# Pairs 6 to 11 of an SSD scan in 32x64 array tiles, a block's two pairs finished together

## The chip, the core and the metric

The kernel runs on one core of one Trainium2 chip, as one launch. A core has a matrix engine (TensorE, PE in the profile, with weight loads listed apart as PEld), VectorE (DVE), ScalarE (ACT), GpSimd (POOL) and a queue that issues most of the transfers (SP). The metric is the device time of one execution in microseconds, the median of several runs. Less is better.

## The reference

Two layers follow each other. The first is a chunked state-space scan over 4 batches x 8 heads x 768 tokens, head dimension 32, state dimension 16. The second is a gated feed-forward layer over all 3072 tokens, 256 -> 1536 -> 256.

```python
# scan, per batch and head, in chunks of 32 tokens (state starts at zero)
cum = cumsum(log(a[chunk]))
M = (Cc @ Bc.T) * exp(cum_i - cum_j) * causal
y = M @ xc + (Cc @ state) * exp(cum)
state = exp(sum(log a)) * state + sum_j(Bc_j xc_j exp(cum_end - cum_j))
# feed-forward over the tokens; the 8 heads x 32 make the 256 features
out = (relu(y @ w_gate) * (y @ w_val)) @ w_out
```

## The kernel before

The kernel takes chunks of 128 tokens, 6 per batch (`NC`). Two chunks are a pair of 256 tokens; there are 12 pairs, 0 to 11, three per batch (`PPB`). Two pairs make a block of 512 tokens, and the feed-forward layer runs over 6 blocks (b = 0 to 5). The decay is folded into B and C, which are scaled by factors from products of `a` that run over a whole pair. So inside a pair a token's output is a masked product of scaled C and B with x, plus scaled C times the carried state.

The scan of one pair p consists of these steps. The names are those of the profile.

- `scale` (L355): GpSimd scales B and C to bf16 and casts x (`to_x`, tile xb). From pair 6 on (`NDMA`) it is `scale_padded` (L278): B and two copies of C go to a tile bz of 6 blocks of 128 columns, each copy of C zero outside the states of its half of the heads, and one DMA transpose from the SP queue turns the six blocks (tile TT). Before pair 6 TensorE transposes do that. Heads are numbered h = 4t + q here: q is one of four 32-row strips of the array, t the half of the strip.
- `G` (L435): the products of C and B. Per chunk four matmuls, one per 32-row strip, each 32x128 in size with 256 moving columns, into four PSUM banks g0 to g3.
- `gevac` (L449): the four banks go, causally masked, to the bf16 tile gs: g0 and half of g1 by ACT (L455, L463) with a mask by GpSimd (L169), the rest by DVE (L466, L470).
- `inter` (L575, matmuls L595): the carried state. Per chunk two full 128x128 matmuls with 128 moving columns into the bank y. The state stands as a block-diagonal tile Sm.
- `Dm` (L599, matmuls L606): gs times x, 16 matmuls per pair in 128x32 tiles, added to the same bank y.
- `yevac` (L613, copies L304): bank y to the bf16 tile yT, by ACT.
- `states` (L532, matmuls L545): the state sums over B and x in the bank A_ps, 4 matmuls per chunk in 128x32 tiles, and `spread` (L553, `spread_one` L509, DVE L514 to L522), which makes Sm from them. Within a batch the sum runs on in PSUM; at the fifth chunk it is multiplied by `over` and continues as `carry`.

The feed-forward layer of block b has 12 slices of 128 hidden features. `gv` (L627) does one slice for 512 tokens: two matmuls of 512 columns for gate (L631), two for val (L634), a relu by ACT (L637) and a product by DVE (L638) into h. `gvh_mm` (L640), `gvh_relu` and `gvh_mul` do the same for 256 tokens, a half tile (L649, L656, L659). `fout` (L671, matmuls L678) multiplies h with w_out, 12 matmuls of 256 columns for 128 tokens, into the bank o, and `foevac` (L696) copies o out (ACT, L706) and issues the store (SP, L707).

PSUM has eight banks: five `shared` ones that gate, val, gv, g0 to g3 and o take in turn, and one each for the tags y, tp and Aps. In the transposes' time tp holds their results.

`in_order` (L15) fixes the order of the instructions on each engine to that of the program, so the loop over b (L859 on) is the schedule. With P = 2b+2, Q = 2b+3 and W = 2b+1 its order from b = 1 on is this:

1. Half tiles for slices 0 to `nh`-1 of the first 256 tokens (`nh` is 6 in block 1, 5 in later ones). At one of them the second pair W of the block is finished: `inter(W)`, `Dm(W)`, `states(P)`, `yevac(W)`, `spread(P)` (L878 to L888). Then half tiles of the same slices for the second 256 tokens.
2. Full `gv` for the remaining slices; `scale` of later pairs on GpSimd.
3. `inter(P)`, `fout(b, 0)`, `G(P)`, `gevac(P)`, `fout(b, 1)`, `foevac`, `fout(b, 2)`.
4. `Dm(P)`, `states(Q)`, `yevac(P)`, `G(Q)`, `spread(Q)`, `gevac(Q)`, `fout(b, 3)`, `foevac` (L962 to L976).

So pair P, the first half of block b+1, is ready a fourth of a block's output work before block b+1 starts, and its partner Q is finished inside block b+1, behind the half tiles of that block's first half.

Of the kernel before, what the change touches and what calls it, by code (L numbers as in the profile page):

```python
# [29 lines left out]
def kernel(  # L30
# [219 lines left out]
    over = const.tile([128, NB], FP32)  # L250

# [13 lines left out]

    yT = glob.tile([128, 2, T], BF16)
# [5 lines left out]
    def zero_padded():  # L272
        for n in range(3):
            z = glob.tile([128, 6, 128], BF16, name="bz%d" % n)
            nc.gpsimd.memset(z, 0.0)
            turned.append(z)

    def scale_padded(p, eng):  # L278

        b, c0, _ = place(p)  # L280
        z = turned[p % 3]
        dst = z.rearrange("s (i k) (q t n) -> s i k t q n", k=3, q=4, t=2)
        src = st[p]["bcr"].rearrange("s i j (t q) n -> s i j t q n", t=2)
        f = fac[:, b, c0:c0 + 2]
        for t in range(2):
            for j in range(2):
                eng.tensor_tensor(  # L287
                    out=dst[:, :, j * (1 + t), t], in0=src[:, :, j, t],
                    in1=f[:, :, j, 4 * t:4 * t + 4].to_broadcast([128, 2, 4, N]), op=ALU.mult)
        st[p]["B"] = [z[:, 3 * i] for i in range(2)]  # L290
        tt = st[p]["TT"] = att.tile([128, 6, 128], BF16, tag="TT", name="TT")
        nc.sync.dma_start_transpose(out=tt, in_=z.rearrange("s k n -> s (k n)"))
# [110 lines left out]
    def bt(p, i, rows):  # L403
        return st[p]["TT"][rows, 3 * i] if p >= NDMA else st[p]["BT"][rows, i]

    def ct(p, i, rows=slice(0, 128), t=None):
        if p >= NDMA:
            c = st[p]["TT"][rows, 3 * i + 1:3 * i + 3]
        elif p < NWIDE:
# [25 lines left out]
    def G(p):  # L435
        s = st[p]
        if "gp" not in s:
            G_banks(p)
        g = s["gp"]
        for i in range(2):  # L440
            for q in range(4):
                r = slice(32 * q, 32 * q + 32)
                nc.tensor.matmul(  # L443
                    out=split(p, g[q][:, i]), lhsT=bt(p, i, r), rhs=ct(p, i, r),
                    start=(i == 0), stop=True, tile_position=(32 * q, 0),
                    skip_group_check=True)
        s["gs"] = att.tile([128, 4, 4, 128], BF16, tag="gs", name="gs", bufs=2)

    def gevac(p, half=True, early=False, between=None, after={}):  # L449
# [19 lines left out]
        if half and not early:  # L469
            nc.vector.tensor_tensor(out=d[:, 1, 0:2], in0=g[1][:, 0:2], in1=m[:, 0:2],  # L470
                                    op=ALU.mult)

# [151 lines left out]

    fst = {}

    def gv(b, f):  # L627
        tk = slice(b * 512, (b + 1) * 512)
        g, v = bank("gate"), bank("val")
        for k in range(2):  # L630
            nc.tensor.matmul(out=g, lhsT=w_tile(wgs, f, k), rhs=yT[:, k, tk],  # L631
                             start=(k == 0), stop=(k == 1))
        for k in range(2):
            nc.tensor.matmul(out=v, lhsT=w_tile(wvs, f, k), rhs=yT[:, k, tk],  # L634
                             start=(k == 0), stop=(k == 1))
# [60 lines left out]
    def foevac(b, ts):  # L696
# [5 lines left out]
        if last:  # L702
# [4 lines left out]
        nc.sync.dma_start(  # L707
            out=out[r0 - 128:r0 + 128, :].rearrange("(i p) m -> p i m", p=128), in_=ob)
# [91 lines left out]
    def turn(p):  # L800
        if p >= NDMA:
            return
        transp(p, 1)
        transp(p, 0)

    def tevac(p, beng, *cengs):
        if p >= NDMA:
            return
# [47 lines left out]
    scale_bc(3, nc.gpsimd)  # L856
    to_x(2, nc.gpsimd)

    for b in range(NBLK):  # L859
        P, Q, W = 2 * b + 2, 2 * b + 3, 2 * b + 1  # L860
        more = P < NPAIR
        for n in (P + 2, P + 3):
            if b and n < NPAIR:
                load(n, nc.sync)

        nh = (4, 6, 5)[min(b, 2)]
        if b == 1:
            zero_padded()
        for f in range(nh):
            if b == 0:  # L870
                continue
            turning = f == (3 if b == 1 else 2)
# [5 lines left out]
            if turning:  # L878
# [3 lines left out]
                if more:  # L882
                    states(P)
                if b == 1:
                    scale_one(P, nc.gpsimd, 1)
                yevac(W, nc.scalar)
                if more:
                    spread(P)  # L888
        for f in range(nh):
            gvh(b, f, 1)  # L890
        for f in range(nh, NF):
            gv(b, f)
# [13 lines left out]
            elif more:  # L906
                if f == max(5, nh):
# [3 lines left out]
                if f == 8:  # L911
                    turn(Q)
                    tevac(Q, nc.scalar, nc.vector)
                    if Q + 1 < NPAIR:
                        scale(Q + 1, nc.gpsimd)
        if more and b:
            inter(P, 0)
            inter(P, 1)
        if b == 0:
# [30 lines left out]
            inter(P, 1)  # L950
        else:
            fout(b, 0)
            foevac(b, 0)
            if more:
                G(P)
                gevac(P)
# [4 lines left out]
        if more:  # L961
            Dm(P)  # L962
            states(Q)
            if b == 0:
                yevac(P, nc.vector)
                G(Q)
                gevac(Q, after={3: lambda: spread(Q)})
                new_bs(Q + 1)
                scale_one(Q + 1, nc.gpsimd, 0)
            else:  # L970
                yevac(P, nc.scalar)
                G(Q)
                spread(Q)
                gevac(Q)
            fout(b, 3, range(6, NF) if b == 0 else range(NF))
            foevac(b, 3)  # L976
        else:
            fout_last(b)
# [32 lines left out]
```

## Time and profile before

| what | value |
|---|---|
| runs before | 123.75, 124.55, 124.83 us; median 124.55 us |
| profiled execution, its own time | 123.81 us |
| its span, first to last instruction | 122.1 us |
| granted TensorE clock | 1.0 |
| DVE, ACT, POOL busy | 74%, 63%, 39% of the span |
| full gate and val matmuls (L631, L634) | 84 + 84, 25.0 us busy each |
| half tile matmuls (L649) | 240, 23.1 + 23.0 us busy |
| output matmuls (L678) | 276, 33.0 us busy |
| DMA transposes (L292) | 6, median 3.0 us from issue to landing |

The profile is of one execution; its own time is 0.74 us below the median of the runs. A matmul's row gives its duration from start to result (273 ns for 256 columns), but matmuls follow each other faster than that, and a group's busy time counts overlapping ones once; the cost of a group is read from the start of it to the start of the next. Blocks 2 to 5 run from 49.2 to about 119 us.

### The profile page before, as it was taken

The page shows a single profiled execution, that of the slowest core. Times are in us where ns is not written, and L with a number is a line of the kernel's source. Part 1 is how long each engine was busy: PE and PEld are TensorE (multiplying, and loading weights), DVE is VectorE, ACT ScalarE, POOL GpSimd, SP SyncE. Part 2 cuts the span into 40 slices and gives each one's busy share as a digit, 9 for nine tenths or more (in the row PEclk, how much of TensorE's full clock was granted, in tenths as well). Part 3 has the DMA queues.
Part 4 walks back from the last instruction along what each step waited for, and adds up shares of the span by engine and source line. Part 5 has one row for each costly group of instructions (what it writes and reads, how often), then busy time and mean ns, then how long its engine had stood idle before and what let it go on. Part 6 is the DMA issues. An engine that isn't in the chain of part 4 may idle for free.

```text
span 122.1 us, 3384 instructions
## 1 busy us (share of the span) xinstructions
PE 118.1 (97%) x1253; PEld 81.5 (67%) x1253; DVE 90.9 (74%) x224; ACT 77.2 (63%) x175; POOL 47.3 (39%) x99
## 2 busy tenths in 40 slices
PE   7999999999999999999999999999999999999990
PEld 2656854677885577884577874677864678854790
DVE  5978879986999855898765998756897657788500
ACT  4167886750988735787645886545987347886240
POOL 6879999043875071904132706033600033000000
PEclk9999999999999999999999999999999999999999
DMA  3999999989979899598962499932320002200022
GB/s 63 209 186 142 180 194 193 213 138 120 166 74 198 111 105 157 177 98 111 128 136 94 107 113 113 162 74 86 116 40 0 0 0 91 86 0 0 0 87 90
DMA packets 79024, 13.31 MB, mean 109 GB/s; under 512 B 71856, under 2 KB 79008, under 8 KB 79008
## 3 DMA queue, kind: packets, MB, share of 16 engines
q1 hardware_dynamic: 71520, 10.15, 51.7%
q0 software_dynamic: 4080, 2.36, 13.7%
q10 hardware_dynamic: 3408, 0.59, 2.5%
q8 instruction: 10, 0.16, 0.6%
q14 instruction: 6, 0.05, 0.1%
HBM read 11.12 MB, written 3.15 MB: 117 GB/s over the span
## 4 chain that ended last, share of the span: by engine, by line
PE 94%; DVE 3%; issue 0%; DVEq 0%
PE o L678 25%; PE gv L649 22%; PE val L634 15%; PE gate L631 15%; PE w L198 4%; PE g L443 3%; PE y L606 3%; PE y L595 2%; PE o L690 1%; PE tp L375 1%; DVE gs L466 1%; DVE bs L330 1%; PE A_ps L545 1%; PE bt L424 1%; PE dw L234 0%; DVE CT L401 0%
## 5 line engine op out<-in xcount | busy, mean ns | idle before, releaser
L638 DVE TENSOR_TENSOR h<-r,val 128x512 bf16<-128x512 bf16 x42 | 28.6, 686 | 6.5 <-ACT r L637 5.5
L678 PE MATMUL o<-wo,h 128*128 128x256 bf16 x276 | 33.0, 273 | 0.0
L637 ACT ACTIVATE r<-gate 128x512 bf16<-128x512 f32 x42 | 25.1, 597 | 9.3 <-PE gate L631 8.8
L678 PEld LDWEIGHTS <-h 128*128 128x128 bf16 x276 | 25.9, 98 | 4.9 <-issue 1.9
L169 POOL TENSOR_SCALAR_AFFINE_SELECT gs<-gs 128x512 bf16<-128x512 bf16 (+1 forms) x24 | 12.2, 529 | 35.3 <-ACT gs L455 35.3
L659 DVE TENSOR_TENSOR h<-r,gv 128x256 bf16<-128x256 bf16 x60 | 23.7, 418 | 2.7 <-ACT r L656 2.1
L634 PE MATMUL val<-yT,wv 128*128 128x512 bf16 x84 | 25.0, 379 | 0.0
L631 PE MATMUL gate<-yT,wg 128*128 128x512 bf16 x84 | 25.0, 379 | 0.0
L656 ACT ACTIVATE r<-gv 128x256 bf16<-128x256 f32 x60 | 22.8, 386 | 2.1
L649 PE MATMUL gv<-yT,wg 128*128 128x256 bf16 x120 | 23.1, 273 | 0.0
L649 PE MATMUL gv<-yT,wv 128*128 128x256 bf16 x120 | 23.0, 273 | 0.0
L466 DVE TENSOR_TENSOR gs<-g,masks 128x512 bf16<-128x512 f32 x24 | 15.4, 684 | 5.2 <-PE g L443 5.2
L634 PEld LDWEIGHTS <-wv 128*128 128x128 bf16 x84 | 8.1, 98 | 10.0 <-DMA wv<-in_moe_w_val_dram 0.3
L455 ACT CAST gs<-g 128x512 bf16<-128x512 f32 x12 | 7.1, 588 | 12.1 <-PE g L443 12.0
L287 POOL TENSOR_TENSOR bz<-bcr,fac 128x128 bf16<-128x128 f32 x24 | 8.9, 402 | 11.6 <-DMA bcr<-in_B_dram 8.0
L631 PEld LDWEIGHTS <-wg 128*128 128x128 bf16 x84 | 8.1, 98 | 7.9
L649 PEld LDWEIGHTS <-wv 128*128 128x128 bf16 x120 | 11.7, 98 | 1.3
L649 PEld LDWEIGHTS <-wg 128*128 128x128 bf16 x120 | 11.2, 98 | 1.8 <-issue 0.2
L706 ACT COPY ob<-o 128x512 f32<-128x512 f32 x11 | 6.5, 587 | 6.3 <-PE o L678 6.3
L304 ACT CAST yT<-y 128x512 bf16<-128x512 f32 (+1 forms) x12 | 6.3, 541 | 5.7 <-PE A_ps L545 3.4
L304 POOL CAST xb<-xr 128x512 bf16<-128x512 f32 (+1 forms) x10 | 5.9, 592 | 5.8 <-DMA xr<-in_x_dram 5.8
L198 PE MATMUL w<-const-bfloat16-1.0 128*128 128x128 bf16 (+2 forms) x27 | 6.3, 378 | 0.8 <-PEq L995 0.8
(109 smaller groups left out, 107.1 us busy)
## 6 DMA issues: line engine op xcount, KB each, us to landing
xr<-in_x_dram SPq DMA_DIRECT2D x23, 128.0 KB, 3.2
out_dram<-ob SPq DMA_DIRECT2D x11, 256.0 KB, 2.3
bcr<-in_B_dram SPq DMA_DIRECT2D x16, 64.0 KB, 2.9
bcr<-in_C_dram SPq DMA_DIRECT2D x16, 64.0 KB, 2.8
wg<-in_moe_w_gate_dram POOLq DMA_DIRECT2D x6, 128.0 KB, 4.9
wv<-in_moe_w_val_dram POOLq DMA_DIRECT2D x6, 128.0 KB, 5.0
wo<-in_moe_w_out_dram POOLq DMA_DIRECT2D x3, 256.0 KB, 7.0
bcr<-in_C_dram SPq DMA_DIRECT2D x3, 128.0 KB, 5.7
```

The lines of the kernel that those rows point to most:

```text
L169: nc.gpsimd.affine_select(out=dst, in_=dst, pattern=pattern, compare_op=ALU.is_ge, fill=0.0, base=0, channel_multiplier=-1)
L198: nc.tensor.matmul(out=w[:, 0:cols], lhsT=nc.const_aps.tensor(1.0, [128, 128], BF16), rhs=nc.const_aps.tensor(1.0, [128, cols], BF16), sta ...
L304: (eng.copy if eng is nc.scalar else eng.tensor_copy)(out=out, in_=in_)
L466: nc.vector.tensor_tensor(out=d[:, q], in0=g[q], in1=m, op=ALU.mult)
L631: nc.tensor.matmul(out=g, lhsT=w_tile(wgs, f, k), rhs=yT[:, k, tk], start=(k == 0), stop=(k == 1))
L634: nc.tensor.matmul(out=v, lhsT=w_tile(wvs, f, k), rhs=yT[:, k, tk], start=(k == 0), stop=(k == 1))
L637: nc.scalar.activation(r, g, AF.Relu)
L638: nc.vector.tensor_tensor(out=fst[b][:, f], in0=r, in1=v, op=ALU.mult)
L649: nc.tensor.matmul(out=gv_[:, j], lhsT=w_tile((wgs, wvs)[j], f, k), rhs=yT[:, k, tk], start=(k == 0 and not (early and j)), stop=(k == 1), ...
L656: nc.scalar.activation(r[:, 0:256], fst[b, f, u][:, 0], AF.Relu)
L659: nc.vector.tensor_tensor(out=fst[b][:, f, u * 256:(u + 1) * 256], in0=fst.pop((b, f, u, "r"))[:, 0:256], in1=fst.pop((b, f, u))[:, 1], op ...
L678: nc.tensor.matmul(out=o[:, ts % 2], lhsT=fst[b][:, f, ts * 128:(ts + 1) * 128], rhs=wo[:, f], start=(f == 0 and new), stop=(f == NF - 1), ...
```

## The change

Pairs 6 to 11 get another layout and another place; pairs 0 to 5 keep theirs.

- `scale_padded` now writes B, C and the two copies of C, 8 blocks instead of 6, with the heads in their natural order (h = 2q + t), in one multiplication and two copies. The transpose turns 8 blocks.
- `G_rows` replaces `G` for these pairs: 16 matmuls instead of 8, each in a 32x64 tile. `inter_rows` replaces `inter`: per chunk four matmuls in 32x64 tiles with 128 columns instead of two full ones. The state then needs no block-diagonal tile, but 64 columns with a mask (tile Sn).
- `Dm_two`, `states_two`, `sums_two` and `yevac_two` do both pairs of a block together. `Dm_two` goes head half by head half (k) through two banks, tags y and tp. `yevac_two` has ACT copy the first bank and DVE the second. `states_two` makes each chunk's sum by itself; `sums_two` adds them up on DVE and masks on GpSimd.
- In blocks 2, 3 and 4 the whole scan of the next block's two pairs lies in the output part, and its copies to yT come two output matmuls before the next block starts. From block 3 on there are no half tiles, and the first slice of a block goes k by k (`turns`). Block 2, which still finishes pair 5, has 8 slices in half tiles instead of 5.
- Block 1 gains `over_sum2` on DVE, three small operations behind `spread(4)`. `zero_padded` moves ahead of the loop. Loads of pairs 8, 9, 10 and 11 and the scaling move earlier in program order; the last store of blocks 2 and 3 is split in two.

```diff
+    def over_sum2(de):
+        own = smask.rearrange("p t (q d) -> p q t d", q=4)[:, :, :, 0]
+        prod = const.tile([128, 2, 8], FP32)
+        for n in range(2):
+            nc.vector.tensor_tensor(
+                out=prod[:, n].rearrange("p (q t) -> p q t", t=2),
+                in0=de[:, (2 + n) * 8:(3 + n) * 8].rearrange("p (q t) -> p q t", t=2),
+                in1=own, op=ALU.mult)
+        nc.vector.tensor_reduce(out=over2[:, 2:4], in_=prod, op=ALU.add,
+                                axis=mybir.AxisListType.X)
...
+    def G_rows(p):
...
+        for i in range(2):
+            for o in range(2):
+                for q in range(4):
+                    r, m = slice(32 * q, 32 * q + 32), slice(64 * o, 64 * o + 64)
+                    nc.tensor.matmul(
+                        out=s["gp"][q][m, i], lhsT=tt[r, 4 * i, m],
+                        rhs=tt[r, 4 * i + 2:4 * i + 4], start=(i == 0), stop=True,
+                        tile_position=(32 * q, 64 * o), skip_group_check=True)
...
+    def inter_rows(p, opened):
...
+            for q in range(4):
+                r, o = slice(32 * q, 32 * q + 32), 64 * (q % 2)
+                nc.tensor.matmul(
+                    out=Y[q // 2][o:o + 64, p % 2, i], lhsT=Sm[r], rhs=tt[r, 4 * i + 1],
+                    start=q not in opened, stop=True, tile_position=(32 * q, o),
+                    skip_group_check=True)
...
+    def Dm_two(ps):
+        for k in range(2):
+            for p in ps:
+                x_, gs = st[p]["x"], st[p]["gs"]
+                for i in range(2):
+                    for c in range(4):
+                        h = 4 * k + c
+                        nc.tensor.matmul(
+                            out=Y[k][32 * c:32 * c + 32, p % 2, i],
+                            lhsT=x_[i][:, h * D:(h + 1) * D], rhs=gs[:, h // 2, 2 * i + h % 2],
...
+    def yevac_two(ps):
+        tk = slice(ps[0] * 256, (ps[1] + 1) * 256)
+        for k, eng in ((0, nc.scalar), (1, nc.vector)):
+            copy(eng, yT[:, k, tk], Y[k].rearrange("q u i m -> q (u i m)"))
...
-        nh = (4, 6, 5)[min(b, 2)]
+        nh = (4, 6, 8, 0)[min(b, 3)]
...
                 if b == 1:
...
                     spread(P)
+                    over_sum2(de)
+                else:
+                    sums_two((P, Q))
...
+        elif more:
+            ahead = (P + 2, Q + 2) if Q + 2 < NPAIR else ()
+            fout(b, 0, range(9))
+            G_rows(P)
+            opened = y_banks()
+            inter_rows(P, opened)
+            inter_rows(Q, opened)
+            gevac(P)
+            fout(b, 0, range(9, NF))
+            fout(b, 1)
+            foevac(b, 1)
+            fout(b, 2, range(6))
+            G_rows(Q)
+            gevac(Q)
+            fout(b, 2, range(6, NF))
+            fout(b, 3, range(10))
+            Dm_two((P, Q))
+            states_two(ahead)
+            yevac_two((P, Q))
+            sums_two(ahead)
+            fout(b, 3, range(10, NF))
+            foevac(b, 3)
+            continue
```

More of the change, by code (lines that the diff above doesn't have):

```diff
@@ L625, with gv @@
+    def yevac_two(ps):
+        tk = slice(ps[0] * 256, (ps[1] + 1) * 256)
+        for k, eng in ((0, nc.scalar), (1, nc.vector)):
+            copy(eng, yT[:, k, tk], Y[k].rearrange("q u i m -> q (u i m)"))
+        for p in ps:
+            st.pop(p)
     fst = {}
-    def gv(b, f):
+    def gv(b, f, turns=False):
+        if b not in fst:
+            fst[b] = ffn.tile([128, NF, 512], BF16, tag="h", name="h")
         tk = slice(b * 512, (b + 1) * 512)
         g, v = bank("gate"), bank("val")
[L630 to L635, printed above, removed]
+        order = [(g, wgs, 0), (g, wgs, 1), (v, wvs, 0), (v, wvs, 1)]
+        for o, ws, k in sorted(order, key=lambda e: e[2]) if turns else order:
+            nc.tensor.matmul(out=o, lhsT=w_tile(ws, f, k), rhs=yT[:, k, tk],
+                             start=(k == 0), stop=(k == 1), skip_group_check=True)
@@ L960 @@
             foevac(b, 2)
[L961 to L976, printed above, removed]
-        else:
-            fout_last(b)
+            fout_last(b)
+            continue
+        Dm(P)
+        states(Q)
+        if b == 0:
+            yevac(P, nc.vector)
+            G(Q)
+            gevac(Q, after={3: lambda: spread(Q)})
+            new_bs(Q + 1)
+            scale_one(Q + 1, nc.gpsimd, 0)
+        else:
+            yevac(P, nc.scalar)
+            G(Q)
+            spread(Q)
+            gevac(Q)
+        fout(b, 3, range(6, NF) if b == 0 else range(NF))
+        foevac(b, 3)
     in_order(tc)
```

141 lines of the change are left out of this document (100 added, 41 removed).

## The prediction

> **What bounds the kernel now.** First the page's busy times, its 40 slices and the chain of waits, to see which engine sets the end:
>
> ```profile
> PE 118.1 (97%) x1253; PEld 81.5 (67%) x1253; DVE 90.9 (74%) x224; ACT 77.2 (63%) x175; POOL 47.3 (39%) x99
> PE   7999999999999999999999999999999999999990
> PE 94%; DVE 3%; issue 0%; DVEq 0%
> ```
>
> From 11 us to the last output tiles the chain is TensorE alone: its stream has no hole, at a full clock. So an instruction taken off PE gives back its whole length, and any new wait of PE costs its whole length. Other engines count only where PE begins to wait for them. Next PE's timeline at the end of block 3 and the start of block 4 (start, us, engine, line):
>
> ```profile
> 77.69 0.59 PE L634 MATMUL val<-yT,wv 128*128 128x512 bf16 x2
> 78.12 0.39 PE L595 MATMUL y<-TT,Sm 128*128 128x128 bf16 x4
> 78.34 1.47 PE L678 MATMUL o<-wo,h 128*128 128x256 bf16 x12
> 79.75 0.40 PE L443 MATMUL g<-TT 32*128 32x256 bf16 x8
> 80.08 2.79 PE L678 MATMUL o<-wo,h 128*128 128x256 bf16 x24
> 82.80 0.41 PE L606 MATMUL y<-gs,xb 128*32 128x128 bf16 x16
> 83.04 0.26 PE L545 MATMUL A_ps<-xb,bz 128*32 128x64 bf16 x12
> 83.23 0.40 PE L443 MATMUL g<-TT 32*128 32x256 bf16 x8
> 83.56 1.48 PE L678 MATMUL o<-wo,h 128*128 128x256 bf16 x12
> 84.88 0.38 PE L649 MATMUL gv<-yT,wg 128*128 128x256 bf16 x2
> ...
> 86.19 0.28 PE L595 MATMUL y<-TT,Sm 128*128 128x128 bf16 x2
> 86.40 0.41 PE L606 MATMUL y<-gs,xb 128*32 128x128 bf16 x16
> 86.63 0.29 PE L545 MATMUL A_ps<-xb,bz 128*32 128x64 bf16 x16
> 86.85 0.39 PE L649 MATMUL gv<-yT,wg 128*128 128x256 bf16 x2
> ```
>
> Starts give the prices. Two of 512 columns take 78.12 - 77.69 = 0.43. Twelve of 256 from 84.88 take 1.31: 0.109 each. Four full ones of 128 columns take 78.34 - 78.12 = 0.22: 0.056 each. `Dm` takes 82.80 to 83.04: 16 matmuls go four at a time, four turns of 0.056. `G` goes four at a time too, so two turns of 0.109, and 0.11 of its 80.08 - 79.75 = 0.33 is something else. The same surplus stands wherever the tile shape changes: 79.75 - 78.34 less 12 x 0.109 = 0.10; 83.23 - 83.04 less three chunks of 0.03 = 0.10; 86.85 - 86.63 less four = 0.10. So a change of tile shape costs 0.10.
>
> Last the neighbours that PE may come to wait for: DVE in block 1; the last product of h and the copy to yT in block 3; the transposes on SP's queue.
>
> ```profile
> 34.04 0.42 DVE L522 TENSOR_TENSOR Sm<-A_ps,smask 128x256 bf16<-128x256 f32 x1
> 34.37 0.28 DVE L514 TENSOR_SCALAR carry<-A_ps,over 128x64 f32<-128x64 f32 x1
> 34.68 0.42 DVE L522 TENSOR_TENSOR Sm<-carry,smask 128x256 bf16<-128x256 f32 x1
> 35.02 2.86 DVE L659 TENSOR_TENSOR h<-r,gv 128x256 bf16<-128x256 bf16 x8
> ```
>
> ```profile
> 78.52 0.69 DVE L638 TENSOR_TENSOR h<-r,val 128x512 bf16<-128x512 bf16 x1 [0.17 <-ACT r L637]
> ```
>
> ```profile
> 83.26 0.58 ACT L304 CAST yT<-y 128x512 bf16<-128x512 f32 x1 [1.08 <-PE y L606]
> ```
>
> ```profile
> 46.47 1.31 SPq L292 DMA_TRANSPOSE TT<-bz  x1
> ...
> 59.49 2.84 SPq L292 DMA_TRANSPOSE TT<-bz  x2
> ```
>
> **What PE saves.** Carried state of pairs 6 to 11: 20 full matmuls x 0.056 = 1.12 become 10 chunks, each one turn of four tiles in different row strips, 0.56: -0.56. Shape changes: seven a block in blocks 2 to 4 (pair W 2, G 2, Dm to G to output 3) and two in block 5, 23 in all; after it 8, 6, 6 and 0, 20 in all: -0.30. State sums: 16 chunk steps become 10, x 0.029: -0.17. Half tiles: a slice costs 8 x 0.109 = 0.874 against 4 x 0.216 = 0.863, and 20 slices become 8: -0.12. `Dm` stays at four turns a pair. `G_rows` stays at two turns if all eight tiles of a chunk run side by side; its later last start (four more starts, some 4 ns apart as inside every group) adds 6 x 0.014 = +0.08. Sum -1.07.
>
> **What PE newly waits for.** At the three block starts. Before, `yevac` ran under half tiles or under `fout(3)`; now the first gate product needs all 512 tokens. ACT's copy began 0.46 behind the first `Dm` matmul (83.26 - 82.80), and in the new order the first bank's half of `Dm_two` is as long as that `Dm`. So yT's first half is there 0.46 + 0.58 + 0.05 (from one engine's end to the next's start) = 1.10 behind it. PE has in that time 0.47 of `Dm_two`, three state steps 0.09, a change 0.10 and two output matmuls 0.22 = 0.88; block 4 has no states, 0.79. Wait 0.22 + 0.22 + 0.31 = +0.75. DVE's copy of the second half starts 0.23 later than ACT's, lasts at most the 0.69 of the other 128x512 operations and is needed 0.43 later, since the slice goes k by k: nothing.
>
> At both `G_rows`, three times. The first begins 9 x 0.109 + 0.10 behind the last val, 78.12 + 1.08 = 79.20; its fourth bank is that of this val, free when the product of 78.52 ends, 79.21 + 0.05: 0.05. The second comes six output matmuls behind `fout(1)`; its fourth bank is the one that `foevac` copies. That copy begins 0.31 behind the last matmul of `fout(1)` (81.60 against 81.29) and ends at 0.90 + 0.05, the tile's turn is at 0.87: 0.07. Sum 3 x 0.12 = +0.35. `Dm_two` follows 16 matmuls behind the second `G_rows`; the last mask on DVE and POOL ended 2.05 behind G's last start in block 3, the tiles that read it start at 2.15: nothing, by a hair.
>
> Block 1. `over_sum2` stands on DVE between the Sm of 34.68 and the eight products from 35.02. Its like in block 0 took 0.34 for one product of 32 elements and 0.10 for the sum; two products and a sum 0.45 to 0.55, say 0.48. The first of the eight frees, at 35.44, the bank of the half tile begun at 33.34, and five banks on PE wants it at 35.54: 0.06 of cover. So +0.42, between 0 (if DVE overlaps them) and 0.50.
>
> Hidden: `sums_two` and the masks (DVE one copy and three sums of 0.25 against two Sm of 0.33 in block 2, where DVE waits for ACT between half tiles; POOL waits 35.3 us in total for the ACT copies); `scale_padded` on POOL (four of 0.36 become, from 0.36 for 128 and 0.58 for 256 elements, one of about 1.0 and two of 0.3); the early memsets (POOL is idle from 21 to 26 us). Without that cover the latter two would cost 0.2 a pair and 3.
>
> Transposes. SP goes from the one at 46.47 (a third longer now) over six loads, two stores and six loads, 0.52 each for the stores and 0.7 to 0.8 for each load, so pair 7's is issued at 57.5 to 59.1, not 59.49. Six blocks landed after 2.7 to 4.1; eight, by 8/6 at most, 2.9 to 5.5. So it lands at 60.4 to 64.6, most likely 61.4. Before, `G(7)` at 65.36 was its first reader; now `inter_rows(7)` is, at about 62.2 (49.6 + 11.2 + 9 output matmuls + 0.4). Taken: 0, since issue and landing have mostly been at their short ends; late end +2.4.
>
> Sum: -1.07 + 0.75 + 0.35 + 0.42 = +0.45. The profiled 123.81 becomes 124.3; it lies 0.74 below the median of the runs, which becomes 125.0. One per cent, 1.25 us, is about what a measurement can tell from no change here.
>
> **Rivals.** (B) The two column halves of a row strip don't run side by side. Rows show strips side by side (L443), column tiles side by side (L606) and both on the diagonal (L586, 32x32, four a turn), but never two column tiles in one strip. Then `G_rows` takes four turns, 6 x 0.22, and the carried state two, 10 x 0.056: +1.87 more, 126.9. Against it: every shape seen overlapped. 0.17.
>
> (C) Pair 7's transpose lands late. From 63.0 on, a wait of 0.8, the kernel is over 1% slower; at 63.2 it is 126.0. For it: the transposes of 86.88 took 4.1 to land on a quieter queue. 0.15.
>
> (D) Tiles of different strips can't write one bank at once; `inter_rows` puts q = 0 and 1 into one. Price 10 x 0.056 = +0.56, 125.5. Against it: L586's 16 matmuls, four strips into one bank, took 13.40 to 13.79 where one by one would be 0.9. 0.05. The Trainium skill, "TensorEngine Tiling (Array Packing)", Gotcha 1: PSUM Pressure, says that different row tiles cannot access the same bank simultaneously. By that rule it would be 125.5; the trace doesn't agree.
>
> (E) The small waits don't come, and `over_sum2` hides: 124.55 - 1.07 + 0.2 to 0.75 = 123.7 to 124.2; only with no wait at all, 123.5. For it: four of my waits are below 0.1. 0.13; over 1% faster 0.05, if changes of shape between small tiles cost less than 0.10.
>
> My forecast has 0.50, own range 124.3 to 125.8. Slower by over 1%: B 0.17, C 0.15 and the upper end of mine 0.04, 0.36; faster 0.05; within 0.59. The range 123.8 to 126.8 leaves out the low half of E and most of B.
>
> **What would show it.** Right: G_rows 0.33 from its start to the next group's besides the carried state, which takes 0.06 a chunk; block 3 some 0.2 shorter than 17.87; a wait of 0.2 to 0.3 before the first gate of blocks 3 to 5; PE 0.4 late at the half tile of 35.54. Wrong: G_rows over 0.5 (B); a hole before `inter_rows` in block 2 (C); no gap at the block starts (E).

## The result, and the profile after

| what | before | after |
|---|---|---|
| median of the runs | 124.15 us (4 runs) | 127.70 us (127.23 to 129.62, 4 runs) |
| ratio, 95% interval | | 1.0271 (1.0220 to 1.0321): slower |
| profiled execution, its own time | 123.81 us | 127.92 us |
| its span | 122.1 us | 126.2 us |

Medians count every run, while ratios, here and below, leave out those of a kernel's runs that took over 1.5% more than its fastest, so a ratio need not be the quotient of two medians.

By the ratio the changed kernel is 3.4 us slower; 0.45 us were forecast, and 127.70 us lies above the range given, 123.8 to 126.8. The page's busy times, its row of TensorE slices and its chain:

```profile
PE 120.2 (95%) x1249; PEld 77.5 (61%) x1249; DVE 89.4 (71%) x214; ACT 74.0 (59%) x160; POOL 52.0 (41%) x105
PE   7899999999999999989989999999999999999990
PE 78%; DMA 6%; SPq 5%; DVE 5%; ACT 2%; issue 1%
```

TensorE has fewer matmuls than before (1249 against 1253) and is still the bound, but its share of the chain fell from 94% to 78%: DMA, SP's queue and DVE are in it now. The view of waits says for what TensorE stood still (us in total, times, longest):

```profile
PE w L198 <- PEq L1134: 0.8, 1, 0.8
PE gv L750 <- ACT yT L316: 0.6, 1, 0.6
PE y L663 <- DMA TT<-bz: 0.5, 1, 0.5
PE tpb L387 <- DVE bs L342: 0.4, 1, 0.4
PE gv L750 <- DVE h L760: 0.2, 1, 0.2
```

The first row is the launch, as long in the kernel before; the fourth is at 5.85 us, ahead of block 0. The timeline shows the other three in their places (start, us, engine, line; idle time and its cause in brackets), and two of the new groups and a block start behind them:

```profile
12.31 0.42 PE L750 MATMUL gv<-yT,wg 128*128 128x256 bf16 x1
12.53 0.37 PE L750 MATMUL gv<-yT,wv 128*128 128x256 bf16 x1
12.73 0.27 PE L750 MATMUL gv<-yT,wg 128*128 128x256 bf16 x1
12.84 0.27 PE L750 MATMUL gv<-yT,wv 128*128 128x256 bf16 x1
...
37.17 0.25 DVE L271 TENSOR_TENSOR prod<-de,smask 128x8 f32<-128x8 f32 x2
37.46 0.17 DVE L275 TENSOR_REDUCE over<-prod 128x2 f32<-128x16 f32 x1
...
38.01 0.38 PE L750 MATMUL gv<-yT,wg 128*128 128x256 bf16 x2 [0.16 <-DVE h L760]
...
55.68 0.29 PE L690 MATMUL A_ps<-xb,bz 128*32 128x64 bf16 x16
...
55.91 0.59 ACT L316 CAST yT<-y 128x512 bf16<-128x512 f32 x1 [0.19 <-PE A_ps L690]
...
56.55 0.38 PE L750 MATMUL gv<-yT,wg 128*128 128x256 bf16 x2 [0.57 <-ACT yT L316]
...
61.91 4.35 SPq L304 DMA_TRANSPOSE TT<-bz  x3
...
64.81 0.29 PE L663 MATMUL y<-TT,Sn 32*64 32x128 bf16 x4
...
65.58 0.30 PE L663 MATMUL y<-TT,Sn 32*64 32x128 bf16 x8 [0.48 <-DMA TT<-bz]
...
83.03 0.48 PE L489 MATMUL g<-TT 32*64 32x256 bf16 x16
83.27 0.40 PE L663 MATMUL y<-TT,Sn 32*64 32x128 bf16 x12
83.61 2.47 PE L779 MATMUL o<-wo,h 128*128 128x256 bf16 x21
...
88.94 0.39 PE L779 MATMUL o<-wo,h 128*128 128x256 bf16 x2
89.38 0.38 PE L735 MATMUL gate<-yT,wg 128*128 128x512 bf16 x1
```

The first four lines are block 0: starts of half tile matmuls are 0.22 apart until 12.7 us and 0.11 after, so the clock was half until there. The record of the granted clock begins, at full, at 12.70 us here and at 6.47 us in the kernel before. At 38.01 TensorE is 0.32 late (start to start, less the 0.218 of two matmuls), at 56.55 0.64, at 65.58 0.64. At 89.38 the block start is 0.22 late.

Where the 4.11 us between the two profiled executions are, by starts of TensorE (a block runs from its first gate or half tile matmul to the next block's, block 5 to the start of the last matmul; differences are of unrounded times):

| | start of block 1 | block 1 | block 2 | block 3 | block 4 | block 5 | last matmul to the end |
|---|---|---|---|---|---|---|---|
| before | 30.94 | 18.24 | 17.84 | 17.87 | 17.78 | 16.29 | 3.15 |
| after | 33.09 | 18.55 | 19.96 | 17.79 | 17.84 | 15.57 | 3.42 |
| difference | +2.15 | +0.32 | +2.11 | -0.08 | +0.06 | -0.72 | +0.27 |

Block 0 and what comes ahead of it hold the same 327 matmuls in both kernels, and yet the largest part is there. Of DMA the page says (issues, KB each, median us to landing):

```profile
xr<-in_x_dram SPq DMA_DIRECT2D x23, 128.0 KB, 3.6
...
bcr<-in_B_dram SPq DMA_DIRECT2D x16, 64.0 KB, 3.5
bcr<-in_C_dram SPq DMA_DIRECT2D x16, 64.0 KB, 3.3
```

Before, these were 3.2, 2.9 and 2.8. The loads are the same in number and size (the page has 11.12 MB read from HBM in both); only those of the later pairs are issued earlier.

### The profile page after: what moved, and what is told of

Its sections match the earlier page's. It is cut to its first block, busy times and chain, and to the rows that moved or that the text cites. A ratio compares the mean times of both kernels' runs of the same rounds, so it can differ in the third digit from the quotient of the medians.

```text
span 126.2 us, 3355 instructions
## 1 busy us (share of the span) xinstructions
PE 120.2 (95%) x1249; PEld 77.5 (61%) x1249; DVE 89.4 (71%) x214; ACT 74.0 (59%) x160; POOL 52.0 (41%) x105
## 3 DMA queue, kind: packets, MB, share of 16 engines
q0 software_dynamic: 4080, 2.36, 13.9%
HBM read 11.12 MB, written 3.15 MB: 113 GB/s over the span
## 4 chain that ended last, share of the span: by engine, by line
PE 78%; DMA 6%; SPq 5%; DVE 5%; ACT 2%; issue 1%
PE o L779 23%; PE gate L735 17%; PE val L735 17%; PE gv L750 7%; SPq L92 3%; DMA bcr<-in_C_dram 3%; DMA TT<-bz 3%; PE w L198 2%; PE g L489 2%; PE g L450 1%; ACT yT L316 1%; PE tp L387 1%; DVE h L760 1%; PE y L628 1%; DVE Sm L544 1%; PE o L791 1%
## 5 line engine op out<-in xcount | busy, mean ns | idle before, releaser
L739 DVE TENSOR_TENSOR h<-r,val 128x512 bf16<-128x512 bf16 x54 | 36.7, 686 | 9.3 <-ACT r L738 6.4
L738 ACT ACTIVATE r<-gate 128x512 bf16<-128x512 f32 x54 | 32.3, 597 | 12.6 <-PE gate L735 11.8
L735 PE MATMUL gate<-yT,wg 128*128 128x512 bf16 x108 | 32.6, 379 | 0.2
L735 PE MATMUL val<-yT,wv 128*128 128x512 bf16 x108 | 32.6, 379 | 0.0
L169 POOL TENSOR_SCALAR_AFFINE_SELECT gs<-gs 128x512 bf16<-128x512 bf16 (+1 forms) x24 | 12.1, 528 | 31.3 <-ACT gs L462 31.3
L735 PEld LDWEIGHTS <-wv 128*128 128x128 bf16 x108 | 10.5, 98 | 13.2 <-issue 0.8
L757 ACT ACTIVATE r<-gv 128x256 bf16<-128x256 f32 x36 | 13.6, 388 | 2.3 <-PE gv L750 0.7
L760 DVE TENSOR_TENSOR h<-r,gv 128x256 bf16<-128x256 bf16 x36 | 13.9, 417 | 1.4 <-ACT r L757 1.2
L750 PE MATMUL gv<-yT,wg 128*128 128x256 bf16 x72 | 14.1, 275 | 0.7 <-ACT yT L316 0.6
L750 PE MATMUL gv<-yT,wv 128*128 128x256 bf16 x72 | 13.9, 274 | 0.0
L295 POOL TENSOR_TENSOR bz<-bcr,fac 128x512 bf16<-128x512 f32 x6 | 6.3, 1058 | 9.0 <-DMA bcr<-in_B_dram 6.2
L750 PEld LDWEIGHTS <-wv 128*128 128x128 bf16 x72 | 7.1, 98 | 0.9
```

The source lines that it names most:

```text
L169: nc.gpsimd.affine_select(out=dst, in_=dst, pattern=pattern, compare_op=ALU.is_ge, fill=0.0, base=0, channel_multiplier=-1)
L735: nc.tensor.matmul(out=o, lhsT=w_tile(ws, f, k), rhs=yT[:, k, tk], start=(k == 0), stop=(k == 1), skip_group_check=True)
L738: nc.scalar.activation(r, g, AF.Relu)
L739: nc.vector.tensor_tensor(out=fst[b][:, f], in0=r, in1=v, op=ALU.mult)
L750: nc.tensor.matmul(out=gv_[:, j], lhsT=w_tile((wgs, wvs)[j], f, k), rhs=yT[:, k, tk], start=(k == 0 and not (early and j)), stop=(k == 1), ...
L757: nc.scalar.activation(r[:, 0:256], fst[b, f, u][:, 0], AF.Relu)
```

## The experiments

**The three waits, one at a time.** The first theory was that the waits of blocks 1 and 2 are the cost, and the late start chance. A plain copy of the kernel before went along:

> The kernel before, unchanged, as a second sample of its start. In the profiles so far PE's full clock was granted 6.5 us into the span before and 12.7 us after, and block 1 began at 30.9 and 33.1 us, though the first 20 us of both programs hold the same instructions. If the late start is a chance of the single execution, this kernel shows it now and then too: block 1 at 32 us or later, or a spread of over 1.5 us among its runs. If it belongs to the changed program, block 1 begins at 30.9 +- 0.3 here again.

Ratio 1.0018 (0.9973 to 1.0064). Its profiled execution, 126.44 us, began block 1 at 33.56 us, with half the clock from 7.2 to 14.0 us, and its runs spread over 2.67 us. So a start as late as the changed kernel's comes in the unchanged kernel too, and a single profile's start proves nothing.

Next, the finish of pair 5 two half tiles sooner:

```diff
-            turning = f == (3 if b == 1 else nh - 1)
+            turning = f == (3 if b == 1 else nh - 3)
```

> The change, with pair 5 finished behind the sixth half tile of block 2 instead of behind the eighth and last. Theory: the 0.64 that PE waits for yT of pair 5 comes from its place at the end of the half tiles, so two half tiles in between (0.87) hide it: no gap there, 0.64 faster than the change, 127.1. Rival: the wait is for DVE's product or a bank, and stays, 127.7.

131.01 us, 1.0488 (1.0410 to 1.0565): slower still, which neither theory had. The wait for yT is gone, but the one for pair 7's transpose grew from 0.64 to 2.07 us, from start to start. Of that growth 0.6 us is what the earlier finish gave; for the other 0.8 the transpose landed 14.7 instead of 13.9 us behind the start of block 2, and why is open. TensorE in the timeline:

```profile
64.11 0.29 PE L663 MATMUL y<-TT,Sn 32*64 32x128 bf16 x4
66.32 0.30 PE L663 MATMUL y<-TT,Sn 32*64 32x128 bf16 x8 [1.92 <-DMA TT<-bz]
66.55 3.95 PE L779 MATMUL o<-wo,h 128*128 128x256 bf16 x21
```

The same 21 output matmuls took 2.47 us in the changed kernel. After that wait the granted clock was half from 67.34 to 70.75 us, so the wait was followed by 1.5 us more of loss.

Then pair 7's transpose issued sooner, by one pair's loads on SP's queue:

```diff
         if b == 2:
-            load(Q + 2, nc.sync)
             scale(Q, nc.gpsimd)
+            load(Q + 2, nc.sync)
```

> The change, with the transpose of pair 7 issued on SP ahead of the load of pair 9 instead of behind it. Theory: the wait of 0.64 before inter_rows of pair 7 is the transpose's landing at 65.54; issued some 5 us sooner it lands near 60 and the wait is gone, 127.1. Rival: the load of pair 9, 1.5 us later now, holds GpSimd and with it the masks of pair 6; then the gap comes back at Dm_two, 127.7 or more.

127.30 us, 1.0217 (1.0146 to 1.0288), which can't be told from the changed kernel's ratio. In the trace the transpose was issued at 56.1 and landed at 61.4, and its wait is gone; block 2 took 19.49 instead of 19.96. A new wait of 0.16 us stands in `Dm_two`, as the rival had it, and GpSimd's timeline explains it:

```profile
64.49 1.06 POOL L295 TENSOR_TENSOR bz<-bcr,fac 128x512 bf16<-128x512 f32 x1 [5.07 <-DMA bcr<-in_B_dram]
...
66.65 1.97 POOL L169 TENSOR_SCALAR_AFFINE_SELECT gs<-gs 128x512 bf16<-128x512 bf16 x4
```

The masks (L169) stand in GpSimd's queue behind the scaling of pair 9, which waits 5.07 us for its load.

All three edits together (both of the above, and `over_sum2` behind slice 10 of block 1):

> The change with both, and with over_sum2 put into the full tiles of block 1 (slice 10) instead of behind spread. The three waits of 0.32, 0.64 and 0.64 go: 1.6 faster than the change, 126.1, blocks 1 and 2 at 18.24 and 18.7 us. What is then left above 124.15 is the start (2.15 in the profile) and the end (0.27), less what blocks 3 to 5 gained. If the start is a chance of the execution, block 1 begins at 30.9 in some profile of these three kernels; if it belongs to the changed program, at 33 in all.

127.63 us, 1.0231 (1.0159 to 1.0303). Block 1 took 18.24 again and block 2 19.10; all three waits are gone, and 0.38 us of a new wait for the masks stands in block 2. The blocks of this profile together are only 0.5 us longer than those of the kernel before, but the ratio is still 2.3% above it. The first theory falls: something outside of the blocks costs more than these waits.

**Where the tiles start in SBUF.** `over2` is a new constant of 16 bytes a partition and takes 32. It lies ahead of the large tiles, so that each of them (B and C, x, TT, bz, ob, the weights, yT, h) starts 32 bytes past a multiple of 64; in the kernel before they start on multiples of 128. The second theory: DMA pieces of 64 and 128 bytes land later on such starts. One kernel each way, and a control:

```diff
     over = const.tile([128, NB], FP32)
+    pad = const.tile([128, 8], FP32)
```

> The kernel before, with an unused constant of 32 bytes a partition behind `over`: every later tile in SBUF starts 32 bytes off a multiple of 64, as in the changed kernel, and nothing else differs. Theory A (the changed kernel's transfers are slow because of where its tiles now start): the first B lands near 4.6 us instead of 3.9 to 4.2, the last store takes 3.6 us or more from issue to landing instead of 3.1, and the time is 0.7 to 1.5 us over the kernel before, the blocks' own lengths (18.24, 17.84, 17.87, 17.78, 16.29) unchanged. Theory B (the late start and the slow end of the changed kernel are the chance of an execution): no change, within 0.4 us.

126.12 us, 1.0075 (1.0024 to 1.0125). In its profiled execution, 126.83 us, all blocks have the lengths of before (18.24, 17.84, 17.87, 17.78, 16.29), block 1 starts at 33.72 and the clock is full only from 12.72 us. The plain copy has shown as late a start, so what speaks for the theory is the ratio, and the first B, which landed at 4.52 us instead of 3.90. The control has `[128, 16]`, 64 bytes:

> The control: the same unused constant with 64 bytes, so that all later tiles move but still start on multiples of 64. Theory A: like the kernel before, within 0.4 us, first B landing at 3.9 to 4.2 us. If this one is slower too, it is the shift itself or the extra tile and not the multiple of 64; theory B expects no change as well.

125.26 us, 1.0024 (0.9983 to 1.0065), no slower than the kernel before, though the interval overlaps that of the 32 bytes. But its first B landed at 4.63 us, not at 3.9 to 4.2: 64 bytes are not enough for that. The same in the changed kernel:

```diff
-    over2 = const.tile([128, NB], FP32)
+    over2 = const.tile([128, 16], FP32)
```

> The changed kernel with its new constant `over2` given 64 bytes a partition in place of 16 (which took 32), so that all later tiles start on multiples of 64 again. Theory A: first landing near 4.0, pair 7's transpose lands about 0.4 us sooner after its issue and the 0.64 us wait for it shrinks, the last store takes 3.1 us; 126.0 to 126.8 in all, 1.0 to 1.6 below the changed kernel. Theory B: no change from it, 127.7.

127.81 us (126.46 to 128.75), 1.0149 (1.0072 to 1.0226, from two of the four runs), and the median is above theory A's 126.0 to 126.8. The wait for pair 7's transpose is gone and block 2 took 19.28, but the first B landed at 4.50. So the next runs put the tiles on multiples of 128, with constants of 128 bytes, `[128, 32]`:

> The kernel before with an unused constant of 128 bytes, so that its tiles start on multiples of 128 as in the kernel before itself (the 64-byte one put them on 64 past a multiple of 128). Theory A2 (a piece of 64 or 128 bytes lands later the less its start is aligned: multiples of 128 best, of 64 next, 32 off worst): the first B lands in about 3.0 us from its issue as in the kernel before, not 3.6, and the time is within 0.3 us of it. Rival (any shift of the tiles costs the same, the alignment does not matter): 3.6 us, and 0.3 to 0.8 us slower.

> The changed kernel with its new constant at 128 bytes, all tiles on multiples of 128. Theory A2: B, C and x land as in the kernel before (medians 3.0, 2.9, 3.2 to 3.4 us), the wait for pair 7's transpose is gone as with 64 bytes (block 2 at 19.3 us), first block starts sooner: 126.0 to 126.8. Rival: as with 64 bytes, 127.0 to 127.8.

The kernel before with the unused 128 bytes: 124.25 us, 0.9999 (0.9959 to 1.0038). The changed kernel on multiples of 128: 126.27 us, 1.0143 (1.0082 to 1.0204), from 1.0271 (1.0220 to 1.0321), by an edit that changes nothing but addresses; the two intervals don't meet. The same three rows of the page for the kernel before, 32 bytes off and then on multiples of 128:

```profile
xr<-in_x_dram SPq DMA_DIRECT2D x23, 128.0 KB, 3.7
...
bcr<-in_B_dram SPq DMA_DIRECT2D x16, 64.0 KB, 3.3
bcr<-in_C_dram SPq DMA_DIRECT2D x16, 64.0 KB, 3.5
```

```profile
xr<-in_x_dram SPq DMA_DIRECT2D x23, 128.0 KB, 3.3
...
bcr<-in_B_dram SPq DMA_DIRECT2D x16, 64.0 KB, 3.0
bcr<-in_C_dram SPq DMA_DIRECT2D x16, 64.0 KB, 2.9
```

So the changed kernel's 3.6, 3.5 and 3.3 come from the starts of its tiles. The landing of the first B, over the profiles of this study: 3.88 to 3.98 us in 11 of 12 kernels on multiples of 128 (4.19 in the copy of before), 4.50 to 4.63 in three on multiples of 64, 4.52 to 4.77 in five that are 32 off. In time, multiples of 64 and of 128 can't be told apart here (1.0024 and 0.9999, 1.0149 and 1.0143).

How much of the late start is the tiles' own? Where the clock was full by 7 us and DVE didn't make TensorE wait in block 0 (such a wait comes below), block 1 began at 30.7 to 31.5 us in six profiles on multiples of 128, at 31.4 and 31.5 in two on multiples of 64, and at 31.5 in the one that is 32 off. The starts at 33.0 to 33.7 are the four with a late clock. So of the 2.15 us between the two profiled executions at most some 0.6 is what the later loads cost by themselves; the rest goes with the late clock.

**Without waits, and aligned.** The version with three edits, 64-byte constant, and GpSimd's scaling of pair 9 behind the half tiles' work, so that the masks come ahead of its wait:

```diff
-                if f == 9:
-                    scale(Q + 2, nc.gpsimd)
-                    load(Q + 3, nc.sync)
-                    load(Q + 4, nc.sync)
+                pass
...
             gevac(P)
+            if b == 2:
+                scale(Q + 2, nc.gpsimd)
+                load(Q + 3, nc.sync)
+                load(Q + 4, nc.sync)
```

> The version with the three single waits taken away (pair 5's finish back two half tiles earlier, pair 7's transpose issued sooner, the doubled `over` behind slice 10 of block 1), plus the 64-byte constant, plus the scaling of pair 9 moved behind the half tiles of block 2, so that GpSimd makes the masks before it waits for pair 9's loads. Theory A: block 1 takes 18.24 us, block 2 18.7 (the masks no longer late), blocks 3 to 5 as in the changed kernel (17.79, 17.84, 15.57), first landing and last store as in the kernel before: 124.2 to 125.2 in all. Theory B (placement does nothing): about 0.4 below the version with three edits, 127.2.

125.72 us, 1.0053 (1.0008 to 1.0097), above theory A's 124.2 to 125.2 and far below theory B's 127.2; blocks 18.23, 18.65, 17.79, 17.84, 15.57, as theory A had them. With 128 bytes:

> The version with the three waits taken away and the masks ahead of GpSimd's wait, now with the constant at 128 bytes. Theory A2: blocks 18.24, 18.65, 17.79, 17.84, 15.57 as with 64 bytes, first landing as in the kernel before: 0.1 to 0.5 below the 64-byte version and within 0.3 us of the kernel before. Rival: equal to the 64-byte version (ratio to the kernel before near 1.005).

125.39 us, 1.0078 (1.0039 to 1.0118): no gain over 64 bytes, against theory A2, and the same blocks except block 1, 18.67. TensorE stood 0.99 us in block 0 and 0.42 in block 1. DVE in block 0, and GpSimd beside it:

```profile
18.55 0.69 DVE L739 TENSOR_TENSOR h<-r,val 128x512 bf16<-128x512 bf16 x1 [0.45 <-PE gate L735]
18.68 2.40 POOL L342 TENSOR_TENSOR bs<-bcr,wfac 128x256 bf16<-128x256 f32 x4
19.15 1.44 DVE L261 TENSOR_TENSOR prod<-de,smask 128x32 f32<-128x32 f32 x1
20.63 0.19 DVE L265 TENSOR_REDUCE over<-prod 128x4 f32<-128x32 f32 x1
...
21.46 0.59 PE L735 MATMUL gate<-yT,wg 128*128 128x512 bf16 x2 [0.83 <-DVE h L739]
```

A product of 32 elements takes 1.44 us. The same product and GpSimd's multiplications in the kernel before:

```profile
18.66 1.89 POOL L330 TENSOR_TENSOR bs<-bcr,wfac 128x256 bf16<-128x256 f32 x3
```

```profile
19.13 0.30 DVE L260 TENSOR_TENSOR prod<-de,smask 128x32 f32<-128x32 f32 x1
```

It takes 0.30 us there, and 0.87 in the changed kernel on multiples of 128. Each time it ends 0.08 us behind the end of one of GpSimd's multiplications, the first of them at 0.30, the second at 0.87, the third at 1.44.

Then the block starts, with `Dm_two` and what follows two output matmuls sooner (`range(8)` for `range(10)` in `fout(b, 3, ...)`):

> The version above with `Dm_two` and what follows it two output matmuls (0.22 us) sooner in blocks 2, 3 and 4, so that four instead of two output matmuls stand between the copies to yT and the next block. If the waits at the block starts are what is left of the change's cost: 0.22 us less at each of the three, 0.09 of wait left at the last, blocks about 18.45, 17.57 and 17.62 instead of 18.65, 17.79 and 17.84; 0.66 below the version above and 0.3 to 0.6 below the kernel before, the one version that beats both. Rival (the masks that end just as `Dm_two` starts then hold it by as much): no change from the version above.

125.17 us, 1.0034 (0.9997 to 1.0072). The three waits at the block starts are gone, but blocks 2 to 4 took 18.64, 17.73 and 17.69: of the 0.66 us only 0.22 came, since `Dm_two` now stands longer for its masks (0.58 from its first matmul to the state step instead of 0.45 in block 3; DVE ends the last mask at 84.61, 0.22 behind the first matmul). The rival was mostly right, and the time is not 0.3 to 0.6 below the kernel before.

**What is left.** First pair 5's finish alone, on multiples of 128:

> The changed kernel on multiples of 128 bytes, with the finish of pair 5 two half tiles sooner and nothing else. On 32-byte starts this edit gained nothing, because PE then waited 2.07 us for pair 7's transpose. Theory: the 0.64 us wait behind the finish of pair 5 is the missed step, and with aligned tiles pair 7's transpose is there in time or nearly: block 2 takes 18.65 to 18.9 instead of 19.27, and the time falls by 0.4 to 0.6. Rival: pair 7's transpose takes the gain back also here: block 2 at 19.3, no change.

125.34 us, 1.0114 (1.0044 to 1.0185), block 2 at 18.65 instead of 19.27: the edit that lost time on misaligned tiles is worth 0.62 us by the trace. The ratio alone, from 1.0143, could not tell.

Then the small products, moved from DVE to GpSimd:

```diff
     nc.scalar.copy(out=de, in_=de_ps)
+    over_sum(de)
+    over_sum2(de)
...
-        nc.vector.tensor_tensor(
+        nc.gpsimd.tensor_tensor(
```

> The version with all waits taken away and the constant at 128 bytes, with the small products for `over` and `over2` made by GpSimd before its own multiplications of pair 3, in place of DVE, which three profiles show held until one of GpSimd's multiplications ends (0.87 to 1.44 us for 32 elements). If this hold is what is left of the distance to the kernel before: no stall in block 0 at 20 to 22 us, block 1 at 18.24, 0.5 to 0.9 below the version with DVE, ratio to the kernel before 1.000 to 1.004. Rival (the end, where the last stores wait behind the fetch of TensorE's instructions, or the start makes it): 0 to 0.3 below.

> The same, with `Dm_two` two output matmuls sooner. Blocks 18.24, 18.64, 17.73, 17.69, 15.57: 0.22 below the version above by block lengths; the end may take up to 0.9 more, if the fetch of TensorE's instructions again begins at the last output matmul. Beats the kernel before only if the end stays at 3.2: 0.2 to 0.3 below it.

> The kernel before, with the small product of `over_sum` on GpSimd in place of DVE. If DVE's hold also comes in some executions of the kernel before, its slower executions go: median 0.1 to 0.4 lower, highest lower. Rival: it comes only with the changed kernel's memsets and loads; no change.

125.66, 125.82 and 124.61 us; ratios 1.0103 (1.0057 to 1.0149), 1.0116 (1.0070 to 1.0161) and 1.0020 (0.9984 to 1.0057). All three misses: GpSimd reached the products only behind its own multiplication, at 19.6 to 19.8 us, DVE waited for them, and TensorE stood 0.79, 0.79 and 0.56 us in block 0 in these profiles. The hold was replaced by a wait, so these runs say nothing of what the hold costs on the mean.

Last the end. In most of these profiles (15 of 20) the last store lands 2.0 to 2.2 us behind the end of the last 16 KB fetch on the queue that brings TensorE's instructions. More and smaller warm-up matmuls at the very start push that fetch forward against the end:

```diff
-    keep_warm(6)
-    keep_warm(1, 384)
+    keep_warm(27, 128)
```

> The kernel before, with the warm-up columns at the very start (6 matmuls of 512 and one of 384) put into 27 matmuls of 128: the same work, 20 matmuls and weight loads more in TensorE's instruction stream, so that its last 16 KB fetch falls some 2 us earlier against the last output matmul. Theory (the last stores land when that fetch has ended, plus 2.1 to 2.3 us): the fetch ends 2 us or more before the last matmul's start, the end shrinks from 3.15 to 2.6 to 2.9 us, time 0.2 to 0.5 us below the kernel before. Rival (the fetch only happens to lie there and the stores take that long by themselves): end 3.1 to 3.2, no change.

> The same edit in the changed kernel with aligned tiles and pair 5's finish two half tiles sooner. Theory: the end shrinks from 3.56 to 2.6 to 2.9 us, 0.6 to 0.9 less time, ratio to the kernel before 1.004 to 1.007. Rival: end stays at 3.4 to 3.6, ratio 1.011.

In the kernel before, 124.58 us, 1.0005 (0.9970 to 1.0040) and an end of 3.17: the fetch ended 1.34 us earlier and nothing came of it. In the changed kernel with aligned tiles and pair 5's finish moved, 125.16 us, 1.0047 (1.0007 to 1.0087), from 1.0114, and an end of 3.02 instead of 3.56. The two intervals overlap, so it is the trace that shows the gain. DMA from 117 to 123 us without the edit (queue: packets, MB, share of 16 engines; then stores, KB each, us to landing), and from 117.3 us on with it:

```profile
q8 instruction: 1, 0.02, 1.4%
...
out_dram<-ob SPq DMA_DIRECT2D x1, 256.0 KB, 3.8
...
out_dram<-ob SPq DMA_DIRECT2D x1, 64.0 KB, 2.1
```

```profile
out_dram<-ob SPq DMA_DIRECT2D x1, 256.0 KB, 2.1
...
out_dram<-ob SPq DMA_DIRECT2D x1, 64.0 KB, 1.5
```

One packet of instructions takes 1.4% of 16 engines over 6 us, 1.34 us of one engine. That the last stores wait behind it on that engine is read from their landings, not seen as such. With the fetch out of the way, the store of 256 KB lands after 2.1 instead of 3.8 us, and the last one 2.12 us behind the last matmul's start instead of 2.64. One rule fits both results, and the last landing of all 20 profiles to 0.12 us: it is 2.12 us behind the last matmul's start, or about 2.1 us behind the fetch's end, whichever is later. In the kernel before the fetch ended 0.18 us ahead of the last matmul's start, just early enough.

No version beats the kernel before. The nearest are the one with early `Dm_two` (1.0034, not told from 1) and the last one (1.0047).

## Why the prediction was wrong, point by point

The sum of +0.45 us holds for the work that it priced. It failed at one term, the transposes put at 0, and it left out three others: where pair 5 is finished, where the new constant puts the tiles, and the end.

**Blocks 2 to 5, right, in part by luck.** Savings of 1.07 less waits of 0.75 and 0.35 at the block starts and at `G_rows` left +0.03 us. In the changed kernel as it stood these blocks took 71.16 us; with the waits that the prediction didn't have away, they took 18.65 + 17.79 + 17.84 + 15.57 = 69.85 us against 69.78: +0.07. The block starts came 0.22, 0.22 and 0.30 late, as forecast. `G_rows` goes in two turns of eight tiles (83.03 to 83.27), and twelve matmuls of the carried state with their change of shape in 0.34 us, so rivals B and D fall. Its two bank waits came as 0.01 and 0.11 us instead of 0.05 and 0.07 (86.00 to 86.44 for the second, less two turns and a change of shape): the same sum, otherwise split. Block 3 by itself became 0.08 us shorter, where some 0.2 was named as a sign, so that the whole fits to 0.04 us is in part luck. The saving is in block 5 (-0.72), which has no scan left to carry, and block 2 pays it back (+0.81), because the scans of pairs 5, 6 and 7 all lie in it.

**`over_sum2`, right in its mechanism.** Forecast 0.42, measured 0.31 (18.55 less 18.24): its two products and the sum held DVE's products of h 0.37 us (37.17 to 37.54) instead of 0.48.

**"Transposes. Taken: 0", wrong.** This is rival C, at 0.15. On the clock of the kernel before (block 2 starts 2.46 us later here), pair 7's transpose was issued at 59.4, later than the range of 57.5 to 59.1, and landed at 63.1, a price of 0.64 us. The step took the early ends of both ranges because "issue and landing have mostly been at their short ends", but the landings were those of the kernel before. On multiples of 128 bytes the changed kernel issued it at 59.0 on the same clock and it landed 3.2 instead of 3.6 us later, at 62.2, 0.1 us ahead of its first reader; there, and on multiples of 64, the wait doesn't come. So the tiles' starts made it late, half at the issue and half at the landing.

**Missed: pair 5's finish.** `turning` in block 2 moved from the third of five half tiles of the first half to the last of eight. Then nothing stands between `yevac(5)` and the half tiles that read it but the state step. No step of the prediction costs this move; it is worth 0.62 us, and the diff's `yevac(W, nc.scalar)` with the rows of block 4 (a copy of 0.58 us) would have given 0.6.

**Missed: the new constant.** The prediction priced `over_sum2`'s work and not its 32 bytes. Aligning the tiles took the ratio from 1.0271 to 1.0143, about 1.6 us. By the two traces 0.69 of it is the transpose's wait in block 2, and the rest lies mostly in the start. In three of five profiles with 32-byte starts the half clock lasted until 12.7 us, in none of three on multiples of 64, and in one of twelve on multiples of 128 (the copy of before, 7.2 to 14.0 us). That later data makes for a later clock fits these few profiles, but wasn't tried by itself, and the plain copy shows that a late clock comes without it.

**Missed: the end.** Taken as unchanged; it was 0.27 us longer in the profiled pair. The last fetch began 0.8 us ahead of the last matmul's start instead of 1.3, and the last stores came behind it. Four matmuls and four weight loads fewer ahead of it would make 0.3 to 0.5 us of that, estimated from the two runs in which 40 more of them moved the fetch by 1.3 and 2.3 us; that this is the reason wasn't tried. Moving the fetch shortened the end by 0.54 us in the traces; the ratios, 1.0114 and 1.0047, differ by some 0.8 us, with overlapping intervals.

The chain of edits closes: 1.0271, aligned 1.0143, pair 5's finish 1.0114, fetch 1.0047. Only the first step is clear of noise in the ratios; the other two, 0.36 and 0.83 us by the ratios, are 0.62 and 0.54 us in the traces. What is left, 0.6 us (0.1 to 1.1), holds the 0.31 of `over_sum2` and the 0.07 of blocks 2 to 5. Rival E fell, since its waits came. Three things stay open: how much of the late start is the tiles' and how much the chance of the clock; what sets the length of that last fetch (0.95 to 1.86 us in these profiles); and why it began 0.1 us behind the last matmul's start in one version with early `Dm_two` and 0.8 us ahead of it in the other.

## What to carry to other kernels

A new constant is also an address: 32 bytes ahead of the large tiles slowed the loads in short pieces here, so compare the tiles' starts, before and after, modulo 64 at least. Cost every line of the diff that moves a copy, not only those that add work, and ask what covers it in its new place. When the waits of a trace don't add up to the difference, look at the parts that the change doesn't touch, the start and the end first.

## What the runs showed of the hardware

- The start of a tile in SBUF counts for transfers in pieces of 64 and 128 bytes: the x loads of SP's queue landed after 3.0 to 3.4 us (medians), the B loads after 2.8 to 3.2 and the C loads after 2.8 to 3.4 in the twelve profiles on multiples of 128, and after 3.6 to 3.9, 3.3 to 3.7 and 3.3 to 3.8 in the five 32 bytes off multiples of 64. The kernel before took 0.75% more (0.24 to 1.25%) for it alone. Loads of the weights, in pieces of 512 and 1024 bytes, took no longer: 4.9, 4.8 and 6.3 us in the kernel before 32 bytes off, 4.9, 5.3 and 7.3 on multiples of 128.
- An fp32 product of DVE with two operands in SBUF, started while GpSimd multiplies, waits for it: 0.30, 0.87 or 1.44 us for 32 elements, each time to 0.08 us behind the end of one of GpSimd's multiplications, which end 0.57 us apart. The Trainium skill, "SBUF — State Buffer", section "SBUF: two separate sides", says that such an operation and a GpSimd one exclude each other for a whole instruction; these rows agree, and show that DVE can lose the turn twice in a row.
- A wait of 2.07 us of TensorE was followed by 3.4 us of half clock, in which 21 output matmuls took 3.95 us instead of 2.47; the two waits of 0.64 us in the changed kernel were not.
- The fetch of TensorE's instructions can delay the last stores by up to 1.1 us (last landing at 3.2 instead of 2.12 us behind the last matmul). The Trainium skill, "Runtime: NRT & Kernel Launch", section "Instruction fetch mechanics", has these fetches as blocks of 16 KiB and calls the cost of crossing into the next one mostly hidden. The trace agrees on the size, and TensorE shows no wait for them, but the last one isn't hidden from the stores.
